# Weight pieces of the experts all on VectorE from the second unit on, and small tiles placed elsewhere

## The chip, the core and the metric

The kernel runs on one core of one Trainium2 chip. The metric is the device time of one execution in microseconds (us), less is better. The engines have the profile's names: PE is TensorE's matmul, PEld its weight load, DVE is VectorE, ACT ScalarE, POOL GpSimd, and SP the engine that issues most DMAs.

## The reference

Three blocks follow each other on 2304 tokens (4 x 576) of width 512, all in float32. What matters here is the third, a mixture of 8 experts that all see every token:

```python
def _moe2_ref(x, w_gate, w1, w2):
    logits = x @ w_gate
    P = np.exp(logits - logits.max())
    for _ in range(8):
        P /= P.sum(1, keepdims=True) + 1e-09
        P /= P.sum(0, keepdims=True) + 1e-09
        P *= N / E
    for e in range(E):
        h = np.maximum(x @ w1[e], 0.0)
        out += P[:, e:e + 1] * (h @ w2[e])
```

Here w1 is 8 x 512 x 1024 and w2 8 x 1024 x 512. Ahead of it stand attention with pooled keys and values, and a dense layer pair of width 2048 with h * cos(h) between.

## The kernel before

A float32 matrix product is made from two float32r halves, high and low: three matmuls (high by high, high by low, low by high). In the experts each product of 2 x 2 blocks is made from seven products of sums of blocks instead of eight (P1 to P7, the Strassen-Winograd scheme; `ORDER`, line 46). So every weight tile goes through a chain before PE may load it: differences of blocks (`combine`), and for each of the seven sums a cut into halves (`halves`, line 964), where ACT rounds to the high half and an elementwise engine subtracts it to get the low one.

The experts' stage runs over 16 units (8 experts by two halves of 1024, `NU`), and in each over 3 pairs of token blocks of 384 (`steps`, line 1595). A step of unit and pair is a first layer (`first_layer`, line 1158: 84 matmuls of 384 columns, stationary the weights whi and wlo, moving the tokens xc) and a second layer (`strassen_layer`, line 1555: 126 matmuls of 256 columns, stationary the activations gh and gl, moving the weights vhi and vlo). PE thus does 252 matmuls of the first sort and 378 of the second in a unit, interleaved. At the first step of a unit `w1_pieces` (line 1358) and `w2_pieces` (line 1394) record the 22 elementwise operations that make its weights: 7 cuts and 4 combines for each layer, all of 128 x 512 elements. They are done while the unit before it is on PE. The tiles carry the names raw (sums of blocks), whi and wlo, vhi and vlo.

Between the layers DVE and ACT turn the first layer's results in PSUM (px, py, pv) into the seven activations: `strassen_result` (line 1486) with the tiles c, s, sf and spare, and cuts into gh and gl. `first_layer` also writes back into PSUM: ACT copies px into py (line 1184), DVE adds py and s into pv (line 1189), and PE accumulates on top, so these two gate PE. The second layer's results (pc, qc) are added to acc by DVE (`accumulate`, line 1534).

Nothing of this order is written out by hand. `Graph.add` records each operation with its engine, an estimate of its duration, and what it reads and writes; `Graph.schedule` (line 273) then places all of them in time by these estimates and emits each engine's instructions in that order. An operation may name two engines, ("V", "G"), and goes to the one that would end it early enough. `VG(n)` (line 442) allows GpSimd where the list `ALONE` holds False, and gives VectorE alone where it holds True. In the loop over the dense layers line 1235 sets it to True for the first four tasks and to False after, and it stays False for the experts. `Graph.schedule` also puts matmuls on the identity (`keep_busy`, line 523, shown as L529) on PE where its plan has a gap of over 0.5 us.

Tiles lie in SBUF in the order in which `Group.open` (line 82) opens their pools, from the left side or from the right. All sizes of large tiles are multiples of 512 bytes of a partition, so that a pool's place within 512 bytes is set by the small tiles ahead of it: sel, lg, cs and the edge tiles.

Of the kernel before, what the change touches and what calls it, by code (L numbers as in the profile page):

```python
# [10 lines left out]
F32 = mybir.dt.float32  # L11
# [12 lines left out]
P = 128  # L24
T = B * S
DM = H * D
KC = DM // P
FU = 512
FC = FU // P
E = 8  # L30
# [3 lines left out]
NT = T // P  # L34
# [6 lines left out]
GW = 32  # L41
# [30 lines left out]
class Group:  # L72
# [9 lines left out]
    def open(self):  # L82
        if self.stack is not None:
            return
        if self.over:
            self.over.open()
        for g in self.after:
            if not g.closed and g.stack is not None:
                g.stack.close()
            g.closed = True  # L90
        self.stack = self.graph.ctx.enter_context(ExitStack())
        if self.name in ("early", "mid"):
            edge = self.stack.enter_context(self.graph.tc.tile_pool(name="edge" + self.name, bufs=1, side=self.side))
            edge.tile([P, 8], F32, name="edge" + self.name)
        for pool in self.pools:
            self.pools[pool] = self.stack.enter_context(
                self.graph.tc.tile_pool(name=pool, bufs=1, side=self.side, reuse_waits="tile"))

# [54 lines left out]
class Graph:  # L153
# [19 lines left out]
    def buf(self, kind, shape, dtype, name):  # L173
        return Buf(kind, shape, dtype, name)
# [264 lines left out]
ALONE = [True]  # L439
# [9 lines left out]
def fused_kernel(ctx: ExitStack, tc: tile.TileContext, qT, kT, kS, vS, v0, k1, v1, wa1, wb1, wa2, wb2, wg, out):  # L449
    nc = tc.nc  # L450
    g = Graph(ctx, tc)
# [3 lines left out]
    base = g.group("base")  # L455
    first = g.group("first")
    second = g.group("second")
    early = g.group("early", "right")
    mid = g.group("mid", "right", (early,))
# [10 lines left out]
    def many(group, pool_name, n, strict=False):  # L470
        return g.kind(group, pool_name, [str(i) for i in range(n)], strict)
# [21 lines left out]
    k_pt = many(early, "ptp", 1)  # L493
    k_ck = {n: g.kind(early, "ck", [n]) for n in ("band", "minus", "kbd0", "kbd1")}
    k_gc = {n: g.kind(mid if n in ("ones", "pr") else base, "gc" + n, [n]) for n in ("ones", "wgr", "sel", "lg", "pr")}
    k_sk = {n: g.kind(mid, "sk", [n]) for n in ("m1", "m2", "nm", "rw", "cs", "cr")}
    k_w2 = many(ahead, "wp2", W2, True)
    k_wd = g.join(k_m, k_cw, strict=True)
    k_wu = g.kind(ahead, "wp2", [str(i) for i in range(10)], True)
# [771 lines left out]
    for u in range(U1):  # L1271
# [16 lines left out]


    gate = {n: buf(k_gc[n], s, F32, n) for n, s in (  # L1290
        ("ones", [P, P]), ("wgr", [P, KC, GW]), ("sel", [P, 6 * E]), ("lg", [P, NT, E]), ("pr", [P, NT, E]))}
    ones, wgr, sel, lg, pr = (gate[n] for n in ("ones", "wgr", "sel", "lg", "pr"))
    add("V", 0.17, lambda: nc.vector.memset(ones.tile, 1.0), [], [ones])
    load(lambda: wgr.tile, lambda: wg, P * KC * GW * 4, writes=[wgr])
# [63 lines left out]
    def w1_pieces(u):  # L1358

        src, w = [], {}  # L1360
        for i in range(2):
            src.append(buf(k_raw, [P, 2, FU], F32, "raw"))
        for i, t in enumerate(src):
            load(lambda t=t: t.tile, lambda i=i: wa2[u, :, i], P * 2 * FU * 4,
                 writes=[(t, 0), (t, 1)] + [(src[1], "room")] * (i == 0))

        def a(i, j):
            t = src[i - 1]
            return (t, j - 1), lambda: t[:, j - 1, :]

        def cut(name, what):
            parts = piece_tiles((k_w1, k_w1), ("whi", "wlo"), [P, FU])
            halves(FU, what[1], what[0], lambda k: parts[k].tile, parts)
            for h in range(2):
                w[name, h] = parts, lambda h=h: [t[:, h * HD:(h + 1) * HD] for t in parts]

        def combine(out, x, y, op):
            tt(VG(FU), out[1], x[1], y[1], op, [b[0] for b in (x, y) if b[0] != out[0]], [out[0]])

        a11, a12, a21, a22 = a(1, 1), a(1, 2), a(2, 1), a(2, 2)  # L1380
        cut("P1", a11)
        cut("P4", a22)
        combine(a22, a21, a22, ALU.add)
        cut("P5", a22)
        combine(a21, a11, a21, ALU.subtract)
        combine(a22, a22, a11, ALU.subtract)
        cut("P6", a22)
        cut("P2", a12)
        cut("P7", a21)
        combine(a12, a12, a22, ALU.subtract)  # L1390
        cut("P3", a12)
        return w

    def w2_pieces(u, goal=FAR):

        src, w = [], {}
        for h in range(2):
            t = buf(k_raw, [P, 2, DM], F32, "raw2")
            src.append(t)
        for h, t in enumerate(src):  # L1400
            load(lambda t=t: t.tile, lambda h=h: wb2[u, :, h], P * 2 * DM * 4,
                 writes=[(t, 0), (t, 1)] + [(src[1], "room")] * (h == 0))

        def b(h, d):
            t = src[h - 1]
            return (t, d - 1), lambda: t[:, :, (d - 1) * HD:d * HD]

        def cut(name, what):
            w[name] = parts = piece_tiles((k_w2, k_w2), ("vhi", "vlo"), [P, FU])
            halves(FU, what[1], what[0], lambda k: parts[k].tile.rearrange("p (g n) -> p g n", g=2), parts,  # L1410
                   goal=goal)

        def combine(out, x, y):
            tt(VG(FU), out[1], x[1], y[1], ALU.subtract, [q[0] for q in (x, y) if q[0] != out[0]], [out[0]])

        b11, b12, b21, b22 = b(1, 1), b(1, 2), b(2, 1), b(2, 2)
        cut("P1", b11)
        combine(b11, b12, b11)
        cut("P5", b11)
        combine(b12, b22, b12)  # L1420
        combine(b11, b22, b11)
        cut("P6", b11)
        cut("P2", b21)
        cut("P7", b12)
        cut("P3", b22)
        combine(b21, b21, b11)
        cut("P4", b21)
        return w
# [37 lines left out]
    def x_loaded(pair):  # L1466

        x = {}
        for name in ORDER:
            t = buf(k_x, [P, 2, 2, NB], F32R, "xc")  # L1470
            load(lambda t=t: t.tile.bitcast(F32), lambda name=name: xc[pair, ORDER.index(name)], P * 4 * NB * 4,
                 reads=[kept_x[pair, name]], writes=[t])
            x[name] = [t], lambda t=t: (t[:, 0], t[:, 1])
        return x
# [153 lines left out]
    boxes = [{} for _ in range(NTP)]  # L1628
    g.lap = False
    for n, (u, pair) in enumerate(steps):  # L1630
        if pair == steps[0][1]:
            w1, w2 = w1_pieces(u), w2_pieces(u, FAR if u else end - 40.0)
        pieces = {}
        first_layer(w1, ready if n == 0 else x_loaded(pair), strassen_result(pieces), goals1[n])
        own = {2: (b_x, b_y)} if n == len(steps) - 1 else None
        strassen_layer(pair, u, pieces, w2, boxes[pair], goals2[n], own)
# [60 lines left out]
```

## Time and profile before

| | |
|---|---|
| median of 3 runs | 1916.88 us (1916.5 to 1919.01) |
| profiled execution | 1917.53 us |
| its span, from the first to the last instruction | 1915.8 us |
| granted TensorE clock | 1.0 over the whole span |
| share of the chain that ended last | PE 85%, DVE 9%, issue 2%, DMA 2%, ACT 2% |
| DMA | 212 GB/s on average |

A page of the profile is read from the busy shares to the chain of work that ended last, and from there to the waits of the engine that the chain names. Where one engine is busy nearly all the time, the few places where it stands still, and the spacing of its own instructions, are all that is left to look at; the other engines matter by when they release it. The experts' stage takes the time from about 497 us to the end, with a period of about 88 us per unit.

### The profile page before, as it was taken

The page shows a single profiled execution, that of the slowest core. Times are in us where ns is not written, and L with a number is a line of the kernel's source. Part 1 is how long each engine was busy: PE and PEld are TensorE (multiplying, and loading weights), DVE is VectorE, ACT ScalarE, POOL GpSimd, SP SyncE. Part 2 cuts the span into 40 slices and gives each one's busy share as a digit, 9 for nine tenths or more (in the row PEclk, how much of TensorE's full clock was granted, in tenths as well). Part 3 has the DMA queues.
Part 4 walks back from the last instruction along what each step waited for, and adds up shares of the span by engine and source line. Part 5 has one row for each costly group of instructions (what it writes and reads, how often), then busy time and mean ns, then how long its engine had stood idle before and what let it go on. Part 6 is the DMA issues. An engine that isn't in the chain of part 4 may idle for free.

```text
span 1915.8 us, 33914 instructions
## 1 busy us (share of the span) xinstructions
PE 1891.6 (99%) x13032; PEld 1850.2 (97%) x13032; DVE 1511.9 (79%) x2720; ACT 1098.1 (57%) x2372; POOL 360.3 (19%) x264
## 2 busy tenths in 40 slices
PE   9999999999999999999999999999999999999999
PEld 7799998899999999999999999999999999999999
DVE  7998856987687777777787787777777877878776
ACT  5875435675566665555556555565555555555653
POOL 0203332252112121212112021212121120212120
PEclk9999999999999999999999999999999999999999
DMA  8856662577665646546546455565465464655553
GB/s 265 245 197 234 237 164 80 196 265 256 232 234 223 239 175 242 223 176 234 217 174 264 168 234 226 191 238 214 179 240 210 181 264 157 245 215 195 234 203 127
DMA packets 104762, 406.76 MB, mean 212 GB/s; under 512 B 11160, under 2 KB 15896, under 8 KB 102552
## 3 DMA queue, kind: packets, MB, share of 16 engines
q1 hardware_dynamic: 102616, 400.01, 56.1%
q0 software_dynamic: 1984, 4.59, 1.4%
q8 instruction: 102, 1.67, 0.4%
q14 instruction: 60, 0.49, 0.1%
HBM read 363.40 MB, written 41.16 MB: 211 GB/s over the span
## 4 chain that ended last, share of the span: by engine, by line
PE 85%; DVE 9%; issue 2%; DMA 2%; ACT 2%; SPq 0%; POOL 0%; POOLq 0%; DVEq 0%; ACTq 0%
PE pc L1565 18%; PE py L1178 15%; PE qc L1565 15%; PE pv L1178 10%; PE px L1178 10%; PE po L989 3%; PE po L991 3%; PE po L990 3%; PE ph L989 2%; PE ph L991 2%; PE ph L990 2%; DVE sf L557 2%; DVE raw L557 1%; DVE gl L557 1%; DVE vlo L557 1%
## 5 line engine op out<-in xcount | busy, mean ns | idle before, releaser
L1565 PE MATMUL pc<-vhi,gl 128*128 128x256 f32 x1152 | 318.2, 276 | 0.0
L1565 PE MATMUL pc<-vlo,gh 128*128 128x256 f32 x1152 | 318.0, 276 | 0.0
L1565 PE MATMUL pc<-vhi,gh 128*128 128x256 f32 x1152 | 318.0, 276 | 0.0
L1178 PE MATMUL py<-xc,whi 128*128 128x384 f32 x1152 | 297.1, 338 | 9.4 <-ACT py L540 5.1
L1565 PE MATMUL qc<-vhi,gh 128*128 128x256 f32 x864 | 238.7, 276 | 0.2 <-DVE qc L557 0.2
L1565 PE MATMUL qc<-vlo,gh 128*128 128x256 f32 x864 | 238.5, 276 | 0.0
L1565 PE MATMUL qc<-vhi,gl 128*128 128x256 f32 x864 | 238.5, 276 | 0.0
L540 ACT ACTIVATE gh<-sf 128x384 fp32r<-128x384 f32 x384 | 195.4, 524 | 63.6 <-DVE sf L557 59.2
L557 DVE TENSOR_TENSOR gl<-sf,gh 128x384 fp32r<-128x384 f32 x384 | 204.0, 561 | 31.8 <-ACT gh L540 31.6
L557 POOL TENSOR_TENSOR raw<-raw 128x512 f32<-128x512 f32 x47 | 62.3, 1326 | 874.3 <-DVE wlo L557 492.2
L1565 PEld LDWEIGHTS pc<-vhi,gl 128*128 128x128 f32 x1152 | 216.2, 188 | 0.1
L1565 PEld LDWEIGHTS pc<-vhi,gh 128*128 128x128 f32 x1152 | 216.2, 188 | 0.1
L1565 PEld LDWEIGHTS pc<-vlo,gh 128*128 128x128 f32 x1152 | 216.2, 188 | 0.0
L1178 PEld LDWEIGHTS py<-xc,whi 128*128 128x128 f32 x1152 | 199.0, 188 | 17.7 <-ACT py L540 10.3
L1178 PE MATMUL px<-xc,whi 128*128 128x384 f32 x768 | 196.4, 336 | 0.2 <-DMA xc<-xc 0.2
L1178 PE MATMUL pv<-xc,whi 128*128 128x384 f32 x768 | 195.9, 336 | 0.0
L1178 PE MATMUL py<-xc,wlo 128*128 128x384 f32 x576 | 192.6, 334 | 0.0
L1565 PEld LDWEIGHTS qc<-vhi,gh 128*128 128x128 f32 x864 | 162.2, 188 | 0.5 <-DVE qc L557 0.5
L1565 PEld LDWEIGHTS qc<-vhi,gl 128*128 128x128 f32 x864 | 162.2, 188 | 0.0
L1565 PEld LDWEIGHTS qc<-vlo,gh 128*128 128x128 f32 x864 | 162.0, 187 | 0.0
L1178 PEld LDWEIGHTS pv<-xc,whi 128*128 128x128 f32 x768 | 132.1, 188 | 0.0
L540 ACT ACTIVATE qc<-pc 128x256 f32<-128x256 f32 x144 | 53.1, 369 | 136.7 <-PE pc L1565 136.6
(245 smaller groups left out, 4671.4 us busy)
## 6 DMA issues: line engine op xcount, KB each, us to landing
xc<-xc SPq DMA_DIRECT2D x357, 768.0 KB, 6.8
wc<-wac SPq DMA_DIRECT2D x112, 256.0 KB, 4.7
raw<-wb SPq DMA_DIRECT2D x32, 512.0 KB, 7.7
raw<-wa SPq DMA_DIRECT2D x32, 512.0 KB, 3.8
raw<-wa SPq DMA_DIRECT2D x8, 1024.0 KB, 7.3
raw<-wb SPq DMA_DIRECT2D x8, 1024.0 KB, 6.0
wac<-m SPq DMA_DIRECT2D x12, 512.0 KB, 6.3
wac<-cw SPq DMA_DIRECT2D x12, 512.0 KB, 3.1
```

Of the source, the lines that this page charges most:

```text
L540: lambda: nc.scalar.activation(out=out(), in_=in_(), func=func, **{k: v() if callable(v) else v for k, v in more.items()}),
L557: (nc.gpsimd if e == "G" else nc.vector).tensor_tensor(out=out(), in0=in0(), in1=in1(), op=op)
L989: nc.tensor.matmul(out=ps, lhsT=lh, rhs=rh, start=(i == 0), stop=False)
L990: nc.tensor.matmul(out=ps, lhsT=lh, rhs=rl, start=False, stop=False)
L991: nc.tensor.matmul(out=ps, lhsT=ll, rhs=rh, start=False, stop=(i == total - 1))
L1178: nc.tensor.matmul(out=ps(), lhsT=l[:, k], rhs=r[:, c, :], start=(start and c + n == 0), stop=(c + n == 3), skip_group_check=True)
L1565: nc.tensor.matmul(out=ps, lhsT=l[:, r], rhs=m[:, k], start=(start and h + n == 0), stop=(h + n == 3), skip_group_check=True)
```

## The change

From the second unit on the experts' weights are made without GpSimd: `ALONE` is True for u > 0, so that `VG` gives VectorE alone for the cuts and combines of `w1_pieces` and `w2_pieces`. The pieces of unit 0 keep the choice. And the small tiles move: the edge tiles ahead of the pools of the groups early and mid (32 bytes each) go, one of 64 bytes comes ahead of pool wp, sel loses 32 bytes, and cs (32 bytes) moves from mid to base, behind lg.

```diff
@@ Group.open
-        if self.name in ("early", "mid"):
-            edge = self.stack.enter_context(self.graph.tc.tile_pool(name="edge" + self.name, bufs=1, side=self.side))
-            edge.tile([P, 8], F32, name="edge" + self.name)
         for pool in self.pools:
+            if pool == "wp":
+                edge = self.stack.enter_context(self.graph.tc.tile_pool(name="edge", bufs=1, side=self.side))
+                edge.tile([P, 16], F32, name="edge")
@@ fused_kernel
-    k_sk = {n: g.kind(mid, "sk", [n]) for n in ("m1", "m2", "nm", "rw", "cs", "cr")}
+    k_sk = {n: g.kind(base if n == "cs" else mid, "gccs" if n == "cs" else "sk", [n]) for n in ("m1", "m2", "nm", "rw", "cs", "cr")}
@@
-        ("ones", [P, P]), ("wgr", [P, KC, GW]), ("sel", [P, 6 * E]), ("lg", [P, NT, E]), ("pr", [P, NT, E]))}
+        ("ones", [P, P]), ("wgr", [P, KC, GW]), ("sel", [P, 5 * E]), ("lg", [P, NT, E]), ("pr", [P, NT, E]))}
@@ the loop over steps
     for n, (u, pair) in enumerate(steps):
+        ALONE[0] = u > 0
         if pair == steps[0][1]:
```

The tiles' places in the built programs, as bytes within 512: before, xc and the first layer's weights both lie at 192, gh and gl at 448, vhi and vlo at 128. After, xc is at 192, the first layer's weights at 256, gh and gl at 0, vhi and vlo at 192. PE loads the next stationary operand while the moving one streams. Counted as the start of the one less the start of the other within 512 bytes, the distances in the experts' stage are:

| loaded while streaming | before | after |
|---|---|---|
| first layer's weights while xc | 0 | 64 |
| gh, gl while vhi, vlo (second layer) | 320 | 320 |
| gh, gl while xc (from first to second) | 256 | 320 |
| first layer's weights while vhi, vlo (from second to first) | 64 | 64 |

The order moves on DVE and ACT. The first place is in the fourth unit, where the second layer's weights are made for the fifth. DVE before (tile numbers are the builder's):

```order
L557 TENSOR_TENSOR qc<-qc,t_10118 128x256
L1550 SCALAR_TENSOR_TENSOR acc_6682<-pc,pr,acc_6682 128x512
L557 TENSOR_TENSOR vlo<-raw_9877,vhi 128x512
L557 TENSOR_TENSOR raw_9877<-raw_9858,raw_9877 128x2x256
L1550 SCALAR_TENSOR_TENSOR acc_6705<-qc,pr,acc_6705 128x512
L557 TENSOR_TENSOR gl<-sf,gh 128x384
L557 TENSOR_TENSOR sf<-sf 128x384
L557 TENSOR_TENSOR gl<-spare,gh 128x384 x2
L557 TENSOR_TENSOR sf<-spare 128x384
L557 TENSOR_TENSOR vlo<-raw_9877,vhi 128x512
L557 TENSOR_TENSOR pv_10237<-py,s_10256 128x384
```

And DVE now:

```order
L557 TENSOR_TENSOR qc<-qc,t_10120 128x256
L557 TENSOR_TENSOR vlo<-raw_9910,vhi 128x512
L1550 SCALAR_TENSOR_TENSOR acc_6694<-pc,pr,acc_6694 128x512
L557 TENSOR_TENSOR sf<-sf 128x384
L1550 SCALAR_TENSOR_TENSOR acc_6717<-qc,pr,acc_6717 128x512
L557 TENSOR_TENSOR gl<-spare,gh 128x384 x2
L557 TENSOR_TENSOR raw_9910<-raw_9902,raw_9910 128x2x256
L557 TENSOR_TENSOR sf<-spare 128x384
L557 TENSOR_TENSOR pv_10238<-py,s_10255 128x384
```

One vlo and one gl have left the stretch ahead of pv, and the combine raw stands later. ACT at the same place before, from sf<-py on:

```order
L540 ACTIVATE sf<-py 128x384
L540 ACTIVATE gh<-sf 128x384
L540 ACTIVATE vhi<-raw_9877 128x512
L540 ACTIVATE py<-px_10222 128x384
L540 ACTIVATE vhi<-raw_9877 128x512
L540 ACTIVATE s_10256<-pv_10237 128x384
```

And now:

```order
L540 ACTIVATE sf<-py 128x384
L540 ACTIVATE gh<-sf 128x384 x2
L540 ACTIVATE py<-px_10223 128x384
L540 ACTIVATE s_10255<-pv_10238 128x384
L540 ACTIVATE vhi<-raw_9910 128x512
```

The two vhi, which read the combine raw, no longer stand ahead of py and of s. The second place is on PE, late in the first unit, in the loop over steps; now:

```order
L1178 MATMUL py<-xc,whi 128x384 x2
L1178 MATMUL py<-xc,wlo 128x384
L1178 MATMUL py<-xc,whi 128x384 x2
L1178 MATMUL py<-xc,wlo 128x384
L529 MATMUL pc<-ident 128x128 x4
L1565 MATMUL pc<-vhi,gh 128x256
L1565 MATMUL pc<-vlo,gh 128x256
```

The row of four matmuls on the identity is new; the experts' stage before has none. On POOL 167 subtractions and additions of the weights (60 vlo, 32 wlo, 75 raw) are gone from its order, and as many have come to DVE.

## Rows read from the trace of the kernel before

**Rows 1.** The page, part 1: busy time, share of the span, instructions.
```profile
PE 1891.6 (99%) x13032; PEld 1850.2 (97%) x13032; DVE 1511.9 (79%) x2720; ACT 1098.1 (57%) x2372; POOL 360.3 (19%) x264
```

**Rows 2.** Waits of PE over the span: who for whom, us in total, times, longest.
```profile
PE py L1178 <- ACT py L540: 5.1, 13, 0.4
PE py L1178 <- DVE pv L557: 4.4, 14, 0.6
```

**Rows 3.** Timeline of PE: start us, us, instruction, count, idle before and its releaser.
```profile
784.06 0.51 PE L1178 MATMUL pv<-xc,whi 128*128 128x384 f32 x2
784.41 0.34 PE L1178 MATMUL pv<-xc,wlo 128*128 128x384 f32 x1
785.14 0.62 PE L1178 MATMUL py<-xc,whi 128*128 128x384 f32 x2 [0.39 <-ACT py L540]
...
789.82 0.28 PE L1565 MATMUL pc<-vlo,gh 128*128 128x256 f32 x1
789.94 0.28 PE L1565 MATMUL pc<-vhi,gl 128*128 128x256 f32 x1
790.51 0.62 PE L1178 MATMUL py<-xc,whi 128*128 128x384 f32 x2 [0.30 <-DVE pv L557]
...
873.08 0.62 PE L1178 MATMUL py<-xc,whi 128*128 128x384 f32 x2 [0.39 <-ACT py L540]
```

**Rows 4.** Timeline of ACT in the same stretch.
```profile
784.07 0.63 ACT L540 ACTIVATE vhi<-raw 128x512 fp32r<-128x512 f32 x1 [1.01 <-DVE raw L557]
784.61 0.47 ACT L540 ACTIVATE py<-px 128x384 f32<-128x384 f32 x1
```

**Rows 5.** Timeline of DVE in the same stretch.
```profile
780.29 0.43 DVE L557 TENSOR_TENSOR qc<-qc,t 128x256 f32<-128x256 f32 x1
...
782.36 1.68 DVE L557 TENSOR_TENSOR raw<-raw,raw 128x512 f32<-128x512 f32 x1
...
785.68 2.13 DVE L557 TENSOR_TENSOR gl<-spare,gh 128x384 fp32r<-128x384 f32 x2
787.74 1.64 DVE L557 TENSOR_TENSOR sf<-spare 128x384 f32<-128x384 f32 x1
...
789.90 0.55 DVE L557 TENSOR_TENSOR pv<-py,s 128x384 f32<-128x384 f32 x1
```

**Rows 6.** Timeline of POOL in the same stretch.
```profile
782.19 1.30 POOL L557 TENSOR_TENSOR vlo<-raw,vhi 128x512 fp32r<-128x512 f32 x1 [1.10 <-ACT vhi L540]
785.71 1.68 POOL L557 TENSOR_TENSOR vlo<-raw,vhi 128x512 fp32r<-128x512 f32 x1 [2.22 <-ACT vhi L540]
787.36 1.60 POOL L557 TENSOR_TENSOR raw<-raw,raw 128x512 f32<-128x512 f32 x1
```

**Rows 7.** Windows, two units: stretch, length, busy us (count) of each engine, clock, DMA.
```profile
593.60:680.50 86.90, 86.90 (x632) 86.72 (x631) 64.33 (x120) 59.10 (x128) 15.17 (x11) 1.00 0.56 216
...
857.00:944.90 87.90, 87.21 (x632) 86.69 (x631) 68.91 (x126) 49.10 (x111) 14.84 (x11) 1.00 0.56 213
```

**Rows 8.** Groups of DVE by form from 680 us on: count, busy us, mean ns.
```profile
L557 DVE TENSOR_TENSOR sf<-spare 128x384 f32<-128x384 f32 x84 | 60.3, 718 | 0.0
...
L557 DVE TENSOR_TENSOR sf<-spare,sf 128x384 f32<-128x384 f32 x83 | 45.5, 548 | 0.0
...
L557 DVE TENSOR_TENSOR raw<-raw,raw 128x512 f32<-128x512 f32 x14 | 23.6, 1686 | 0.5
L557 DVE TENSOR_TENSOR raw<-raw 128x512 f32<-128x512 f32 x27 | 18.6, 689 | 0.6
```

**Rows 9.** Groups of PE by form over the span: count, busy us, mean ns.
```profile
L1565 PE MATMUL pc<-vhi,gl 128*128 128x256 f32 x1152 | 318.2, 276 | 0.0
...
L1178 PE MATMUL px<-xc,whi 128*128 128x384 f32 x768 | 196.4, 336 | 0.2 <-DMA xc<-xc 0.2
...
L1178 PE MATMUL px<-xc,wlo 128*128 128x384 f32 x384 | 128.3, 334 | 0.0
...
L529 PE MATMUL psc<-ident 128*128 128x128 f32 x12 | 1.5, 275 | 0.0
```

## The prediction

> **What bounds the kernel now.** I read the busy shares first: PE is busy for 1891.6 us, 99% of the span [rows 1]. That leaves two sources of gain, the places where PE stands still and the spacing of its own matmuls; no other engine's busy time counts by itself. So the next view is PE's waits [rows 2]. Two sorts recur: py waits 13 times for ACT and 14 times for pv from DVE, 9.5 us together, nearly all of it in the experts' stage. The timeline of PE shows that they return with the units: the wait for ACT at 785.14 us comes again at 873.08, one period of 87.94 us later [rows 3].
>
> What such a wait costs is more than its idle time. From one matmul's start to the next there pass 0.73 us (784.41 to 785.14), where two ordinary steps take 0.35 (784.06 to 784.41), so 0.175 each: 0.555 lost. The two matmuls behind it then take 0.62 instead of 0.51, another 0.11: **0.67 us** for the wait on ACT. The same reading at 789.94 to 790.51 gives 0.57 against 0.12, and again 0.11: **0.56 us** for the wait on DVE [rows 3]. A unit thus loses 1.23 us.
>
> Who is late? ACT wrote py at 784.61 only, because a vhi stood ahead of it in its order and waited 1.01 us for DVE's raw [rows 4]. That raw took 1.68 us on DVE [rows 5], where the same 128 x 512 operation from one buffer takes 0.69 on average [rows 8]. The timeline of POOL has a vlo from 782.19 on, 1.30 us long, that ends at 783.49; the raw began at 782.36 and ended at 784.04, just 0.55 after POOL was through [rows 5, 6]. The second wait has the same origin: the pair gl took 2.13 us and sf<-spare 1.64 [rows 5], while POOL worked on vlo until 787.39 and on raw until 788.96 [rows 6]; alone, an operation of that size takes 0.55 (sf<-spare,sf in [rows 8]). In this stretch DVE loses 0.99 + 1.03 + 1.09 = 3.1 us of the 9.6 between qc and pv to POOL, and pv is late by some 0.5.
>
> **The change part by part.** The sums are made against the profiled execution, 1917.53 us, of which the span is 1915.8; the median of the runs is 0.65 us below it.
>
> *GpSimd's share to VectorE.* POOL's order loses 167 operations, 11 a unit [rows 7]. With them goes what stretches DVE. At the first wait, ACT's order now has py ahead of both vhi, so py does not depend on DVE's raw at all. At the second, DVE's order from qc to pv has one vlo and one gl less, and nothing in it can be stretched by POOL: 3.1 + 0.7 + 0.55 = 4.3 us less work ahead of a pv that must come 0.5 earlier. I therefore drop both waits: 13 x 0.67 + 14 x 0.56 = 16.5 us, and as the longest wait on pv was 0.6 where the usual one is 0.30 [rows 2, 3], 0.3 more: **-17 us**. Bounds: 0, were the lateness from elsewhere, and -17.
>
> *VectorE's own load.* It takes 11 more operations of 0.69 us a unit [rows 7, 8], 7.6 us. DVE was busy for 68.9 of 87.9 us in a unit [rows 7], with at least the 3.1 us of stretch in it, so it goes to about 73.4, or 76.5 without any relief. Cover: 19 us of idle time a unit. Were that cover gone, each operation would cost up to its 0.69. What queues behind a weight piece on DVE is the next pv, c, qc or acc, and PE waits for the first three; the plan sees the pieces now at durations that nothing stretches, and puts them between. **0**.
>
> *ScalarE, SP, POOL.* No DMA is added or removed; ACT does the same roundings in another order. Nothing after unit 0 waits for POOL any more. 0.
>
> *The unit where the plan changes over.* Late in the first unit four matmuls on the identity stand in PE's order, so the planner sees PE idle there: the pieces of the second unit are already all on DVE while the first steps fill it. The row of such matmuls has 12 records in 1.5 us [rows 9]; PE's order of before has six there, so each leaves two records, and four are 8 records and 1.0 us. If they lie in a gap that is there anyway they cost 0; if the gap is longer than they are, half a microsecond more. **+1 us**.
>
> *The small tiles.* They move no work. What they change is where the weights being loaded lie against the data streaming, 0 to 64 bytes in the first layer, 256 to 320 from the first to the second. A first-layer matmul with whi takes 336 ns on average, one with wlo 334 [rows 9]; if that difference were all due to the distance, 48 steps x 56 matmuls with whi x 2 ns = 5.4 us would come back. Against it: wlo has the same distance 0 and is not longer. The other bound is 0. A loss has no support: 320 is what the second layer has all along, and 64 is its last matmul's distance to the first layer, and those rows keep their 276 ns [rows 9]. Neither bound is nearer, so I take a value between, **-2 us**.
>
> [...]
>
> Sum: -17 + 1 - 2 = -18, so 1917.53 - 18 = 1899.5 for a profiled execution, and 0.65 less for the median: **1898.9, say 1899 us**.
>
> **The rivals.** *The distances change nothing.* For: wlo at distance 0 shows no excess [rows 9]. Then only the waits go: 1901 us.
>
> *The wait on ACT stays.* For: ACT executes in order, and another late input could stand ahead of py. Against: the new order has only gh<-sf there, which it also had before. It gives back 13 x 0.67 = 8.7: 1907.7 us.
>
> *The change does not do what it says.* PE's waits would come from the order of the chain itself and POOL's work be only beside it. For: the unit from 593.6 us on, in which POOL does 11 operations too, has no such loss (86.90 us against 87.90) [rows 7], so GpSimd's work alone is not enough to make the waits. Against: the stretched operations end exactly behind POOL's. Both waits stay: 1899 + 17 = 1916 us, no change.
>
> *Slower: VectorE becomes late for pv.* A unit has six pv (three steps, two halves), each a release of PE. With 7.6 us more work on DVE, several could come late by one piece. Each costs 0.56 as measured. At more than two a unit the gain is spent (1.23 / 0.56 = 2.2); if all six came late, 3.4 us a unit against 1.23 now, 14 units x 2.1 = 30 us more: about 1946 us. For: DVE would be at 83% to 87%, and the planner put fillers on PE when the pieces moved. Against: that is in one place of the first unit only, and in the later units it planned none.
>
> **How the numbers follow.** Forecast, waits gone and part of the spacing back: 0.54 (1899). Distances worth nothing: 0.26 (1901). The wait on ACT stays: 0.09 (1907.7). No change: 0.05 (1916). Slower: 0.06 (1946). The lower end is the forecast with the full 5.4 us for the distances and the fillers free: 1899 - 3.4 - 1 = 1894.6. The first two cases hold 0.80, their own range reaches from 1894.6 to about 1903 (1901, the fillers' half microsecond, and one short wait here and there); since some of their chance lies outside it, I reach up to the third case: 1894 to 1907. About 0.2%, 3.8 us, is what a measurement of this kernel can tell from no change. Faster by more than that: 0.54 + 0.26 + 0.09 = 0.89; within it 0.05; slower 0.06.
>
> **What would show it.** PE's waits on ACT's py and on DVE's pv gone from the list in the experts' stage, and the period of a unit 86.6 to 86.8 us instead of 87.94. The groups sf<-spare and gl<-spare on DVE at 0.55 us and raw<-raw,raw at 0.69 on average. DVE busy about 73 us in a unit, with 137 operations, none on POOL. The first layer's matmuls: whi at 334 shows the distances to matter, at 336 not. The fillers at the end of the first unit, about 1 us. Wrong would be the forecast if PE's list had new entries on DVE's qc, c or pv, or if raw<-raw,raw stayed long with POOL idle.

## The result and the profile after

The changed kernel takes 1898.11 us (median of 4 runs, 1893.01 to 1900.43), the kernel before in the same comparison 1917.81 (1916.5 to 1919.01). The ratio is 0.9895, with the interval 0.9876 to 0.9915: 1.05% faster. The forecast was 1899.0. The profiled execution below is the one of 1893.01 us, with a span of 1891.3.

The page of the changed kernel, busy shares and chain:

```profile
PE 1878.7 (99%) x13040; PEld 1845.6 (98%) x13040; DVE 1537.8 (81%) x2888; ACT 1089.9 (58%) x2371; POOL 135.0 (7%) x97
...
PE 93%; DVE 4%; ACT 1%; DMA 1%; issue 0%; SPq 0%; POOL 0%; ACTq 0%
```

POOL has 97 instructions instead of 264 and DVE 2888 instead of 2720 [rows 1]. DVE's share of the chain that ended last falls from 9% to 4%: the pieces of DVE's work that stood between POOL and PE are out of it.

PE's waits over the span of the changed kernel begin with these (who for whom, us in total, times, longest):

```profile
PE psc L529 <- POOL ident masks.py:199: 2.1, 1, 2.1
PE ptr L883 <- ACT vs L540: 0.8, 1, 0.8
```

Both lie ahead of the experts. The two entries of 13 and 14 waits [rows 2] are gone, and nothing of DVE's or ACT's has come in their place: from 500 us on the view lists no wait of PE at all. A unit in the middle of the stage (length, then busy us and count of PE, PEld, DVE, ACT, POOL, clock, DMA):

```profile
1200.00:1286.52 86.52, 86.52 (x632) 86.52 (x631) 70.62 (x136) 48.57 (x111) 0.00 (x0) 1.00 0.58 216
```

PE is busy for the whole of it; the window before of 87.90 us had 87.21 [rows 7]. DVE, with the 11 operations of POOL on top, is busy for only 1.7 us more.

How the stretch ahead of pv looks now, on DVE (start, us, instruction, count, idle before and its releaser):

```profile
777.67 1.02 DVE L557 TENSOR_TENSOR gl<-spare,gh 128x384 fp32r<-128x384 f32 x2
778.60 0.68 DVE L557 TENSOR_TENSOR raw<-raw,raw 128x512 f32<-128x512 f32 x1
779.20 0.55 DVE L557 TENSOR_TENSOR sf<-spare 128x384 f32<-128x384 f32 x1
780.18 0.57 DVE L557 TENSOR_TENSOR pv<-py,s 128x384 f32<-128x384 f32 x1 [0.43 <-ACT vhi L540]
```

These are the instructions of [rows 5]: the pair gl takes 1.02 us instead of 2.13, raw 0.68 instead of 1.68, sf<-spare 0.55 instead of 1.64. Where pv came late, DVE now stands idle for 0.43 us ahead of it, waiting for ACT. ACT in the same stretch:

```profile
777.12 0.94 ACT L540 ACTIVATE gh<-sf 128x384 fp32r<-128x384 f32 x2
778.03 0.47 ACT L540 ACTIVATE py<-px 128x384 f32<-128x384 f32 x1
779.07 0.49 ACT L540 ACTIVATE s<-pv 128x384 f32<-128x384 f32 x1 [0.56 <-PE pv L1178]
779.46 0.62 ACT L540 ACTIVATE vhi<-raw 128x512 fp32r<-128x512 f32 x1
```

No vhi stands ahead of py, and none waits 1.01 us for raw [rows 4].

Groups of DVE by form from 680 to 1880 us (count, busy us, mean ns), to be held against [rows 8]:

```profile
L557 DVE TENSOR_TENSOR wlo<-raw,whi 128x512 fp32r<-128x512 f32 x91 | 62.5, 687 | 12.8 <-ACT whi L540 11.0
...
L557 DVE TENSOR_TENSOR sf<-spare 128x384 f32<-128x384 f32 x83 | 45.8, 551 | 0.0
...
L557 DVE TENSOR_TENSOR raw<-raw,raw 128x512 f32<-128x512 f32 x42 | 28.7, 683 | 0.0
```

Groups of PE over the span, against [rows 9]:

```profile
L1565 PE MATMUL pc<-vhi,gl 128*128 128x256 f32 x1152 | 318.0, 276 | 0.0
...
L1178 PE MATMUL px<-xc,whi 128*128 128x384 f32 x768 | 194.9, 335 | 0.0
...
L1178 PE MATMUL px<-xc,wlo 128*128 128x384 f32 x384 | 128.7, 335 | 0.0
```

The whole span falls by 24.5 us, the median of the runs by 19.7. To see what belongs to the change, I take the experts' stage alone, from the first to the last matmul px<-xc,whi. The view of one tile's instructions gives both starts, before:

```profile
L1178 PE MATMUL px<-xc,whi x768: 334/334/445, 496.8 to 1890.3; 128*128 128x384 f32 x192
```

and after:

```profile
L1178 PE MATMUL px<-xc,whi x768: 332/335/441, 492.4 to 1865.8; 128*128 128x384 f32 x192
```

That is 1393.5 us before and 1373.4 after, so **-20.1 us in the stage**, the part that the change touches. The other 4.4 us of these two profiles lie ahead of it; a second profile of the change, below, begins its stage 3.0 us later than this one, and the last section shows that most of the 4.4 belongs to the execution, not to the change. The same two numbers for the experiments are in the tables below as "stage". "Unit" is the period after which an instruction of the stage returns, as 865.12 to 951.64 us for raw<-raw,raw on DVE in the changed kernel.

### The profile page after: what moved, and what is told of

It reads as the page before. It is cut to its first block, busy times and chain, and to the rows that moved or that the text cites. A ratio compares the mean times of both kernels' runs of the same rounds, so it can differ in the third digit from the quotient of the medians.

```text
span 1891.3 us, 33781 instructions
## 1 busy us (share of the span) xinstructions
PE 1878.7 (99%) x13040; PEld 1845.6 (98%) x13040; DVE 1537.8 (81%) x2888; ACT 1089.9 (58%) x2371; POOL 135.0 (7%) x97
## 4 chain that ended last, share of the span: by engine, by line
PE 93%; DVE 4%; ACT 1%; DMA 1%; issue 0%; SPq 0%; POOL 0%; ACTq 0%
PE pc L1565 21%; PE py L1178 17%; PE qc L1565 16%; PE pv L1178 11%; PE px L1178 11%; PE po L989 3%; PE po L991 3%; PE po L990 3%; PE ph L989 2%; PE ph L991 2%; PE ph L990 2%; DMA raw<-wa 1%; DVE xd L557 0%; PE ptr L883 0%; PE px L897 0%; PE psc L776 0%
## 5 line engine op out<-in xcount | busy, mean ns | idle before, releaser
L1178 PE MATMUL py<-xc,whi 128*128 128x384 f32 x1152 | 293.0, 335 | 0.0
L540 ACT ACTIVATE gh<-sf 128x384 fp32r<-128x384 f32 x384 | 190.1, 522 | 29.6 <-DVE sf L557 27.0
L1178 PEld LDWEIGHTS px<-xc,whi 128*128 128x128 f32 x768 | 128.3, 188 | 0.6 <-issue 0.6
```

The costliest lines, as they stand in the source:

```text
L540: lambda: nc.scalar.activation(out=out(), in_=in_(), func=func, **{k: v() if callable(v) else v for k, v in more.items()}),
L1178: nc.tensor.matmul(out=ps(), lhsT=l[:, k], rhs=r[:, c, :], start=(start and c + n == 0), stop=(c + n == 3), skip_group_check=True)
```

## The experiments

My theory after the result: GpSimd's reads made VectorE's two-input operations late, those made py and pv late, and that is nearly all; the tiles give about two microseconds. Its rivals: the gain comes from the new order of the instructions, or from the tiles. All ratios are against the kernel before on the same chip.

### One half of the change each

Without the tiles (the diff of the change without `Group.open`, `k_sk` and sel):

```diff
     for n, (u, pair) in enumerate(steps):
+        ALONE[0] = u > 0
```

> VectorE alone from the second unit on, small tiles where they were: the instruction order of the change, the distances of before (0 in the first layer, 256 from the first to the second). If the distances cost PE its spacing: no waits on py or pv, but a unit of 86.6 to 86.8 us instead of the change's 86.52, so 2 to 4 us over the change in all, about 1901 us. If they cost nothing (the spacing was lost by something that GpSimd's work did): a unit of 86.52 us and the time of the change, 1898 us.

Measured: 1899.48 us, ratio 0.9909 (0.9894 to 0.9924), stage 1375.6, unit 86.68 (869.60 to 956.28). PE's waits on py and pv are gone. Its groups of PE:

```profile
L1178 PE MATMUL px<-xc,whi 128*128 128x384 f32 x768 | 196.5, 337 | 0.0
...
L1178 PE MATMUL px<-xc,wlo 128*128 128x384 f32 x384 | 128.5, 335 | 0.0
```

The tiles alone (the change without the line with ALONE):

```diff
     for n, (u, pair) in enumerate(steps):
-        ALONE[0] = u > 0
```

> Small tiles moved, GpSimd keeps its share: the instruction order of before, the distances of the change. If the distances cost PE its spacing: the two waits of a unit stay, and a unit is 87.94 - 0.19 = about 87.75 us, 3 us under before in all, about 1914.5 us. If they cost nothing: 87.94 us a unit and 1917.5 us. If the tiles were the whole of the change: 1898 us.

Measured: 1917.63 us, ratio 1.0006 (0.9994 to 1.0019), stage 1393.0, unit 87.77. The waits stay:

```profile
PE py L1178 <- ACT py L540: 5.2, 13, 0.4
PE py L1178 <- DVE pv L557: 2.9, 14, 0.6
```

The line with ALONE brings nearly the whole gain. The tiles are below what the total time can tell: between the change and the kernel without its tiles the unit is 0.16 us shorter and the stage 2.2. In the profile of the tiles alone a unit is 0.17 us shorter than before (87.77 against 87.94). Counted from the first px<-xc,whi of one unit to that of the next, however, the fourth and the fifth took 89.27 and 88.59 us there (87.94 and 87.92 before), which covers it in the stage; why these two are longer is open. The excess that the tiles remove is in whi: 337 ns against 335 for wlo without them, 335 for both with them.

### Is it GpSimd's reading, or the order?

Here the order of every engine is that of the kernel before, and the tiles too; only what GpSimd executes for the weights from the second unit on is another instruction, so these weights are not computed. One that only writes:

```diff
         def run(e=how["engine"]):
+            if e == "G" and late:
+                nc.gpsimd.memset(out().bitcast(F32), 0.0)
+                return
             (nc.gpsimd if e == "G" else nc.vector).tensor_tensor(out=out(), in0=in0(), in1=in1(), op=op)
...
     for n, (u, pair) in enumerate(steps):
+        LATE[0] = u > 0
```

> The kernel before with its instruction order and its tiles, but from the second unit's weights on GpSimd writes zeros with a memset in place of each subtraction or addition (so the experts' weights are not computed). If GpSimd's reads stretch VectorE's operations and these make PE wait: sf<-spare, gl<-spare and raw<-raw,raw fall to 0.55, 0.55 and 0.69 us, both waits of a unit go, 86.7 us a unit, 17 us under before: 1900 us. If the order is what makes PE wait: the waits stay, 87.9 us a unit, 1917 us. If a write alone blocks VectorE too: in between, with operations stretched by the length of the memset, some 0.5 us.

Measured: 1898.67 us, ratio 0.9905 (0.9879 to 0.993), stage 1375.1, unit 86.69. The waits on py and pv are gone. Where the combine was held up before, the memset now begins behind it:

```profile
866.15 0.69 DVE L563 TENSOR_TENSOR raw<-raw,raw 128x512 f32<-128x512 f32 x1
...
866.40 0.52 POOL L561 MEMSET vlo<- 128x512 f32 x1 [0.73 <-PE qc L1571]
```

So this place cannot tell whether a write that begins first would hold raw up. One in the second unit can:

```profile
604.89 0.53 POOL L561 MEMSET raw<- 128x512 f32 x1
604.90 0.69 DVE L563 TENSOR_TENSOR raw<-raw,raw 128x512 f32<-128x512 f32 x1
```

raw keeps its 0.69 us beside it. The groups of DVE, 680 to 1880 us:

```profile
L563 DVE TENSOR_TENSOR sf<-spare 128x384 f32<-128x384 f32 x84 | 46.3, 552 | 0.0
...
L563 DVE TENSOR_TENSOR raw<-raw,raw 128x512 f32<-128x512 f32 x14 | 9.7, 693 | 0.5
```

This is the clearest result of the study: with not one instruction moved, raw takes 693 ns instead of 1686 and the stage is 18.4 us shorter. So the new order was not needed for either wait; vhi may stand ahead of py on ACT, as long as the raw that it reads is in time. That reading is what counts is not yet shown by it. A memset reads nothing, but it is also shorter than the subtraction it replaces (0.52 us against 1.30 to 1.68), and so it is seldom in the way: of DVE's some 970 operations with both inputs in SBUF from 590 us on, 77 began beside an operation of GpSimd and over 0.15 us ahead of its end in the kernel before, and 3 here. So a short operation that does read was tried beside it:

```diff
+            if e == "G" and late:
+                nc.gpsimd.tensor_copy(out=out(), in_=in0())
+                return
```

> As the memset experiment, but with a copy of the first input on GpSimd, which reads SBUF once instead of twice (weights not computed either). If any read of SBUF by GpSimd shuts out VectorE's operation with two inputs in SBUF: sf<-spare and gl<-spare stay above 0.6 us on average, by as much as the copy is long, and PE's waits stay in part: 1902 to 1916 us. If only two reads do: 0.55 us, no waits, 1900 us.

Measured: 1898.79 us, ratio 0.9903 (0.9883 to 0.9922), stage 1375.7. One wait of PE is left, and the timeline has its cause:

```profile
868.46 0.61 POOL L561 CAST vlo<-raw 128x512 fp32r<-128x512 f32 x1 [0.55 <-PE qc L1571]
868.48 1.13 DVE L563 TENSOR_TENSOR raw<-raw,raw 128x512 f32<-128x512 f32 x1
...
870.72 0.62 PE L1184 MATMUL py<-xc,whi 128*128 128x384 f32 x2 [0.19 <-ACT py L541]
```

The copy began 0.02 us ahead of raw and ended at 869.07; raw ended at 869.61, 0.54 later, and py was late once. A unit on, raw takes 0.69 again (at 955.28). So here a read of GpSimd that began first held the operation up until it was over, although it took only 0.61 us.

The time is not the one that was expected of a read (1902 to 1916 us). Like the memsets, the copies are seldom in the way: 6 operations began as above, and sf<-spare and gl<-spare keep 552 and 554 ns on average. The mechanism therefore shows in the rows, not in the time of these two runs: all 6 ended 0.41 or 0.54 us behind the copy, and none of the 3 beside a memset was held up. In these runs the subtractions do harm because they read and, at 1.30 to 1.68 us, also last long enough to be in the way. A long operation that only writes was not tried.

### Which weights?

Both are the change with ALONE True for one layer's weights only, from the second unit on:

```diff
-        ALONE[0] = u > 0
...
-            w1, w2 = w1_pieces(u), w2_pieces(u, FAR if u else end - 40.0)
+            ALONE[0] = u > 0
+            w1 = w1_pieces(u)
+            ALONE[0] = False
+            w2 = w2_pieces(u, FAR if u else end - 40.0)
```

> The other half: VectorE alone only for the first layer's weights. If the waits come from GpSimd's work on the second layer's weights: both waits stay, a unit of 87.75 us (87.94 less the distances' 0.17), and the four matmuls on the identity come in the first unit: about 1916 us. If any GpSimd operation in a unit makes waits in proportion to its number: half the waits gone, 1907 us.

Measured: 1914.21 us (10 runs, 1910.33 to 1920.02), ratio 0.9996 (0.9985 to 1.0007), stage 1390.6, unit 87.78; PE's waits stay:

```profile
PE py L1178 <- ACT py L540: 5.8, 14, 0.4
PE py L1178 <- DVE pv L557: 4.0, 14, 0.3
```

Its POOL at the place of the first wait:

```profile
780.61 1.32 POOL L557 TENSOR_TENSOR vlo<-raw,vhi 128x512 fp32r<-128x512 f32 x1 [1.08 <-ACT vhi L540]
```

and its DVE:

```profile
780.78 1.70 DVE L557 TENSOR_TENSOR raw<-raw,raw 128x512 f32<-128x512 f32 x1
```

The other way round:

```diff
-        ALONE[0] = u > 0
...
-            w1, w2 = w1_pieces(u), w2_pieces(u, FAR if u else end - 40.0)
+            w1 = w1_pieces(u)
+            ALONE[0] = u > 0
+            w2 = w2_pieces(u, FAR if u else end - 40.0)
+            ALONE[0] = False
```

> The change, but VectorE alone only for the second layer's weights (vlo and their combines), while GpSimd keeps its choice for the first layer's (wlo). Both waits of a unit lie where the second layer's weights are made. If that is what counts: no waits, a unit of 86.52 us, and without the planner's four matmuls on the identity late in the first unit about 1.5 us under the change, 1896.5 us. If GpSimd's work on wlo makes waits of its own: 87 to 88 us a unit.

Measured: 1895.64 us (1895.06 to 1895.99), ratio 0.9894 (0.9879 to 0.9908), stage 1372.9, unit 86.62 and 86.52 (866.68, 953.30, 1039.82). A unit of it:

```profile
766.40:852.92 86.52, 86.52 (x632) 86.52 (x631) 69.69 (x133) 48.97 (x110) 5.10 (x4) 1.00 0.57 216
```

POOL still does four operations a unit, of the same sort and about as long, and PE loses nothing, although DVE's wlo takes 947 ns on average there. In the kernel above, with the first layer's weights alone, POOL did seven. The number differs too, but the second unit of the kernel before has eleven without a wait [rows 7]. So what counts is not how much GpSimd does, but where: the second layer's weights are made beside the chain raw, vhi, py and beside gl, sf, pv, where VectorE has no time to spare.

### The unit where the plan changes over

The changed kernel's matmuls on the identity in the first unit (from the view of line 529: count, ns min/median/max, first and last start):

```profile
L529 PE MATMUL pc<-ident x8: 271/275/275, 577.1 to 577.9; 128*128 128x128 f32 x8
```

They are the eight records that were forecast. Starting the new rule one unit later removes them:

```diff
-        ALONE[0] = u > 0
+        ALONE[0] = u > 1
```

> The change from the third unit on (u > 1) in place of the second. The first unit keeps the order of before, without matmuls on the identity. If these and the order around them cost 1.5 us in the first unit: 1.5 us under the change, 1896.5 us, with units of 86.5 us from the second on. If the plan of the first unit costs nothing: 1898 us.

Measured: 1896.22 us, ratio 0.9899 (0.9884 to 0.9913), stage 1372.6, unit 86.52, no such matmuls in the first unit. Against the change (stage 1373.4, and 1373.1 in a second profile of it, below) the plan of the first unit costs 0.5 to 0.8 us. In total time neither this kernel nor the one with the second layer's weights alone can be told from the change.

### Other distances

Four kernels are the change with one small tile more or one of another size. Three of them put an edge ahead of the group mid, which of PE's operands moves vhi and vlo alone; shown with 48 elements (192 bytes), the others have 16 and 32:

```diff
         self.stack = self.graph.ctx.enter_context(ExitStack())
+        if self.name == "mid":
+            low = self.stack.enter_context(self.graph.tc.tile_pool(name="low", bufs=1, side=self.side))
+            low.tile([P, 48], F32, name="low")
```

> The change with an edge of 192 bytes ahead of the group mid, so that vhi and vlo lie at the same place within 512 bytes as gh and gl: distance 0 in the second layer, 256 from the second to the first; the first layer keeps 64. If distance 0 costs any matmul what it cost the first layer's (0.16 us for 252 in a unit, 0.65 ns each): 378 x 0.65 ns = 0.25 us a unit, 86.75 us. If it costs only where the moving rows are 384 long: 86.52 us.

> As the experiment with the second layer at 0, but with an edge of 64 bytes in the group mid: 384 in the second layer, 128 from the second to the first, 64 and 320 for the rest as in the change. If only 0 hurts: 86.52 us a unit. If an edge in that group alone slows PE (the first layer was slower in that experiment at its own 64): 87 to 90 us.

> The same with an edge of 128 bytes: 448 in the second layer, 192 from the second to the first. If only 0 hurts: 86.52 us a unit. If the loss grows as the weights' start comes near the data's start within 512 bytes: between 86.52 and 89.7 us, over that at 384.

The fourth halves the edge ahead of wp:

```diff
-                edge.tile([P, 16], F32, name="edge")
+                edge.tile([P, 8], F32, name="edge")
```

> The change with an edge of 32 bytes instead of 64 ahead of pool wp: 32 in the first layer and from the second to the first, 288 in the second and from the first to the second. If only a distance of 0 hurts: 86.52 us a unit. If the distance must be over 32 bytes: more, at most the 89.7 us of the second layer at 0.

Measured, with the order of all engines the same and no recurring wait on PE in any:

| distances: first layer / second layer / first to second / second to first | unit | stage | time | ratio to before |
|---|---|---|---|---|
| 64 / 320 / 320 / 64 (the change) | 86.52 | 1373.4 | 1898.11 | 0.9895 (0.9876 to 0.9915) |
| 0 / 320 / 256 / 64 (tiles of before, waits gone) | 86.68 | 1375.6 | 1899.48 | 0.9909 (0.9894 to 0.9924) |
| 64 / 448 / 320 / 192 | 88.33 | 1401.6 | 1925.4 | 1.0057 (1.0043 to 1.0071) |
| 32 / 288 / 288 / 32 | 88.53 | 1404.4 | 1928.47 | 1.0065 (1.0041 to 1.0089) |
| 64 / 384 / 320 / 128 | 89.16 | 1414.0 | 1936.17 | 1.0105 (1.0082 to 1.0129) |
| 64 / 0 / 320 / 256 | 89.72 | 1422.8 | 1944.18 | 1.0147 (1.0127 to 1.0167) |

The last three rows stand for two runs each, the one with 448 for six. The kernel with the second layer at 0, groups of PE:

```profile
L1568 PE MATMUL pc<-vhi,gl 128*128 128x256 f32 x1152 | 325.6, 283 | 0.0
...
L1181 PE MATMUL px<-xc,whi 128*128 128x384 f32 x768 | 199.6, 340 | 0.0
...
L1181 PE MATMUL px<-xc,wlo 128*128 128x384 f32 x384 | 129.8, 338 | 0.0
```

The second layer's matmuls go from 276 to 283 ns, most of what the unit shows (378 x 7 ns = 2.6 of its 3.2 us). But the first layer's grow as well, from 335 to 340 and 338, although its own distance is 64 in both kernels. So the distance between two operands is not the whole mechanism. Nor is it a few late matmuls: from one start to the next the median goes from 113 to 119 or 120 ns in the second layer, and from 173 to between 176 and 178 in the first. An edge of 64 bytes, with no instruction moved, costs 38 us here (1936.17 against 1898.11), nearly twice what the whole change gains. That the places matter is shown; by what rule is left open, and that they are counted within 512 bytes is my choice, which no run tests. An edge ahead of mid moves vhi and vlo, and with them sf, c, s, t and pr, which lie on the same side, against everything else in SBUF at once, and the distance from second to first layer together with that in the second; these runs don't separate the two.

### The change once more

No edit: the changed kernel on another chip, to see how far two profiles of the same kernel differ.

> The change itself once more, for a second profile. If its profiled execution's 3.3 us within the first 17 us of the span and 1.3 us at one wait of PE near 298 us were chance: a span of 1894 to 1899 us with the same units of 86.52 us. If they belong to the change: 1891 us again.

Measured: 1896.89 us (1892.95 to 1900.39), ratio 0.9901 (0.9877 to 0.9925), stage 1373.1, 0.3 us from the first profile. Its span is 1894.2, 2.9 us longer: the difference lies ahead of the stage (see the last section).

## Why the prediction was right

**The sum.** It was -18 against the profiled execution; the stage lost 20.1 and the medians 19.7. The time lies 0.9 us below the 1899.0 forecast, well inside the scatter of its own runs. The parts as measured below, -18.4, +0.5 to +0.8 and -2.2, add up to -19.8 to -20.1.

**The waits, -17.** Right, and for the reason given: the run with memsets keeps order and tiles and gains 18.4 in the stage. The reading of a wait by the spacing of starts held: 0.67 + 0.56 = 1.23 a unit against 87.94 - 86.69 = 1.25 measured. Over 14 units that is 17.5; the other 0.9 of the 18.4 stands in the third and the thirteenth unit, which took 88.52 and 88.33 us before (counted by the first px<-xc,whi) and 86.71 and 86.69 with the memsets. So the gain passed the bound of -17, which had only 0.3 for waits longer than the usual. Two steps of the argument were true but idle: that py stands ahead of vhi in ACT's new order, and that one vlo and one gl have left DVE's stretch ahead of pv. In the run with memsets neither holds, and both waits go all the same.

**The first unit, +1.** Measured 0.5 to 0.8: the sign right, the size somewhat smaller.

**The small tiles, -2.** Right in size, by luck: -2.2 in the stage, where -2 was picked between the bounds 0 and -5.4 with nothing to choose by. What was claimed beside it, that only a distance of 0 shows an excess and that "a loss has no support", held for the places that the change uses and is wrong as a rule: 32 / 288, 384 and 448 cost more than the change gains. The safe part of the argument was that both new distances were already in use in the rows of before; nothing more could be read from them. My test for it, whi at 334 or 336, was poorly put: whi and wlo both came out at 335, and it is their difference, 2 ns before and 0 now, that shows it. With clock, order and waits the same, the unit differs by 3.2 us with the place of the tiles, so they are not worth nothing. Whether it is the weight load that costs is not shown by these runs.

**VectorE's load, 0.** Right: no new wait. But 73.4 us a unit was expected and 70.6 came, and two terms were mis-sized. I added 0.69 for each operation; back to back, each adds about 0.61, as durations overlap (a pair vlo takes 1.29 in the changed kernel where one takes 0.68): 6.7 instead of 7.6. And I counted the 3.1 us of stretch of one place only. The groups of the kernel before, 680 to 1880 us, have another:

```profile
L557 DVE TENSOR_TENSOR wlo<-raw,whi 128x512 fp32r<-128x512 f32 x65 | 59.8, 920 | 19.7 <-ACT whi L540 19.7
```

wlo took 920 ns where it takes 687 now: 65 x 0.233 = 15.1 us over about 14 units, 1.1 a unit more. With both, 68.9 + 6.7 - 3.1 - 1.1 = 71.4, and 0.8 stays unexplained.

**The rivals.** The distances worth nothing was 1901; the kernel without the tiles took 1899.48. The wait on ACT, 1907.7, did not stay. "No change" rested on the second unit, from 593.6 us on, where POOL does 11 operations without a loss. That observation was right, and the timeline of the kernel before says why it did not count. POOL and DVE there:

```profile
604.41 1.31 POOL L557 TENSOR_TENSOR vlo<-raw,vhi 128x512 fp32r<-128x512 f32 x1
606.30 0.69 DVE L557 TENSOR_TENSOR raw<-raw,raw 128x512 f32<-128x512 f32 x1
610.43 1.31 POOL L557 TENSOR_TENSOR vlo<-raw,vhi 128x512 fp32r<-128x512 f32 x1 [4.71 <-ACT vhi L540]
610.45 0.57 DVE L557 TENSOR_TENSOR pv<-py,s 128x384 f32<-128x384 f32 x1 [0.39 <-ACT vhi L540]
```

In that unit no work of POOL lies beside raw, which takes 0.69 us, and pv, which reads py in PSUM, is not held up by the vlo beside it (0.57 us). In these runs GpSimd's work costs only beside the operations that py and pv wait for. "Slower" by late pv did not come: DVE waits 0.43 us ahead of the pv shown above.

## What to carry to other kernels

When a two-input operation on VectorE takes twice its usual time, as raw did here with 1.68 us instead of 0.69, look at what GpSimd reads at that moment, and follow the late result to the engine that bounds the kernel. Moving the work to VectorE left it hardly busier here (70.6 us of a unit instead of 68.9), and only the pieces near such a chain had to move. Where PE has no idle time left, compare the spacing of its matmuls between builds: a small tile ahead of a pool cost 1.4% to 2.4% against the change in these runs, so check the places of the operands after every change of the tiles.

## What the runs showed of the hardware

**In these traces a read of GpSimd that begins first holds an operation of VectorE with two inputs in SBUF off entirely.** The operation ends a fixed time after GpSimd's, as if it began only then: 0.55 us for 128 x 512 in the kernel before (783.49 to 784.04), 0.54 beside the copy, and 0.55 in the run with the first layer's weights alone (781.93 to 782.48). In the kernel before this holds for all 76 that were stretched by over 0.06 us from 590 us on: 43 of 128 x 512 ended 0.55 us behind GpSimd's and 33 of 128 x 384 between 0.41 and 0.42. Its length thus depends on when GpSimd ends, not on itself. An operation with one of its inputs in PSUM was not held up (pv above, 0.57 us): in the kernel before 131 of them began beside an operation of GpSimd from 590 us on and over 0.15 us ahead of its end, and none took over 0.02 us more than the shortest of its sort. GpSimd was held up in its turn: its vlo at 785.71, begun 0.03 us behind DVE's gl, took 1.68 us instead of 1.30 [rows 5, 6].

**Small tiles of 32 to 192 bytes, which move other tiles, changed the spacing of float32r matmuls**, by up to 3.2 us in 86.5 over a unit, while the granted clock is between 0.999 and 1.000 over all these kernels. I had expected 5.4 us for the whole kernel at most; it was up to 49 between the best and the worst stage (1373.4 and 1422.8).

**The first matmuls of an execution ran at about half their later speed, one in 213 ns instead of 111, for a time that differed between executions.** The timeline of PE in the first profile of the change:

```profile
8.47 3.59 PE L529 MATMUL psc<-ident 128*128 128x72 f32 x24
11.89 2.17 PE L741 MATMUL psc<-kbd,q 128*128 128x144 f32 x16
```

The second profile of the change:

```profile
8.48 1.33 PE L741 MATMUL psc<-kbd,q 128*128 128x144 f32 x4 [0.82 <-DMA q<-qt]
9.60 5.24 PE L529 MATMUL psc<-ident 128*128 128x72 f32 x24
14.63 3.35 PE L741 MATMUL psc<-kbd,q 128*128 128x144 f32 x16
```

And the kernel with VectorE alone for the first layer's weights, where PE waits for nothing at this place:

```profile
8.56 5.23 PE L529 MATMUL psc<-ident 128*128 128x72 f32 x24
13.59 4.14 PE L741 MATMUL psc<-kbd,q 128*128 128x144 f32 x16
```

The same 24 matmuls on the identity take 3.6 or 5.2 us, the sixteen behind them 2.2 to 4.1. Taken one by one, those of 72 columns start every 213 ns and those of 144 every 240 up to a certain moment, and every 111 and 123 ns from then on; the ratio is 1.9. The moment is at 10.1 us in the first profile of the change and 16.4 in the kernel before; from the rows shown it is at about 17.0 in the second profile, and past 17.2 in the last one, where all sixteen still start at the slow spacing. At just 10.12 and 16.40 us the records of the granted clock begin in the traces of the first two, with full speed; of the stretch ahead there is no record, and the 1.00 that the views print for it shows nothing. That the clock is the cause is therefore an inference, not a reading. PE had been at work since 2.06 us in all four. A wait does not decide it: PE waited 0.43 us for the first tokens in the kernel before and 0.82 in the second profile, but for nothing in the last one, which was slow for the longest time of the four. From 10.1 to 16.4 us at half the speed loses about 3.1 us, most of the 4.4 by which the two profiles differ ahead of the experts. The same kernel does the one and the other, so it is no part of the change. What sets the moment was not tried.
